# Layer norm 2 and attention weights transposed by DMA instead of TensorE, with held fc1 loads and row-wise weight loads

## The chip, the cores and the metric

The kernel runs on one core of one Trainium2 chip. The metric is the device time of one execution in microseconds (us). The span of a profile is about 1.8 us shorter than the time of the same run. Engines: PE (TensorE matmuls), DVE (VectorE), ACT (ScalarE), POOL (GpSimd), SP (SyncE, which issues the loads).

## The reference

One diffusion-transformer block, in bf16, with B = 2 sequences of N = 256 tokens, D = 1152, two heads and an MLP of F = 4608:

```python
h = layernorm(x) * (1 + scale_a) + shift_a
q, k, v = split(h @ wqkv)
attn = softmax(q @ k.T * Dh ** -0.5)
x = x + gate_a * ((attn @ v) @ wo)
h2 = layernorm(x) * (1 + scale_m) + shift_m
return x + gate_m * (gelu(h2 @ w_fc1) @ w_fc2)
```

The shifts, scales and gates come from `silu(c) @ w_mod`. The 512 tokens are four token tiles of 128 (t = 0, 1 are b = 0; t = 2, 3 are b = 1). D is nine blocks of 128, numbered k. This kernel lays the dimension that a matmul sums over on the partitions. So the attention weights and the normalized h2, which are made with tokens on the partitions, are transposed before they enter attention-times-V and fc1: 16 and 36 blocks of 128 x 128.

## The kernel before

The parts that matter, cut. Weight matrices are loaded as column panels (runs of 768 B) or, for `w_mod`, as groups of rows (runs of 2304 B), in pieces of 864 KB. SP issues the loads in order, each when its buffer is free (the longest wait of a load for PE in the trace is 15.5 us):

```python
def load_section(name, s):                       # row-wise
    for r in range(0, KD, 3):
        nc.sync.dma_start(w[:, r:r + 3, :], wmod_v[:, r:r + 3, s * D:(s + 1) * D])
def load_panels(name, view, col0):               # column panels, PW = 384
    for n in range(NPD):
        nc.sync.dma_start(w[:, :, n * PW:(n + 1) * PW], view[:, :, col0 + n * PW:...])
```

Attention weights are transposed on PE, 16 blocks of 128 x 128, then copied out of PSUM:

```python
for b in range(B):
    for h in range(H):
        pTt = acc_tile([P, TPB, N], "pTt", BF16)
        for qt in range(TPB):
            for kc in range(TPB):
                nc.tensor.transpose(pTt[:, kc, ...], attn_tiles[(b, h, qt)][...], ident[:])
        evac(attnT, pTt[:])
```

Layer norm 2: statistics of x1 on DVE, normalization on ACT and DVE, then 36 transposes on PE that are mixed as "filler" among the wo matmuls (for b = 0) and the fc1 matmuls (for b = 1). The modulation (scale and shift per feature) is done while PSUM is drained:

```python
def ln2_transpose(b, ks, eng):
    pt = aux_tile([P, len(ks), N], "pt", BF16)
    ...  nc.tensor.transpose(pt[:, i, ...], xn2[b * TPB + tl][:, k * P:(k + 1) * P], ident[:])
    ...  # ACT or DVE: hT[:, k, b] = pt * scale_m[k, b] + shift_m[k, b]
```

fc1 works on the first MSPLIT = 10 of its 36 output blocks once for b = 0 (256 columns), then once for b = 1, so that it can start while b = 1 is still being normalized. The other blocks take all 512 tokens at once.

## Time and profile before

| | before |
|---|---|
| time, median of runs | 250.13 us |
| attention-times-V starts | 77.88 us |
| wo starts | 82.24 us |
| fc1 starts | 100.79 us |
| fc2 starts | 174.41 us |
| span ends | 248.30 us |

The stage starts are those of the first matmul of each stage in the trace. First the page of the kernel before: the span, PE's busy time with its share of the span and number of instructions, and the shares of the chain of waits that ended last.

```profile
span 248.3 us, 4032 instructions
...
PE 239.7 (97%) x1734; PEld 144.9 (58%) x1745; DVE 63.9 (26%) x172; ACT 69.1 (28%) x135; POOL 30.8 (12%) x46
...
PE 91%; DMA 3%; ACT 2%; DVE 1%; issue 1%; SPq 0%; ACTq 0%; DVEq 0%
```

PE is busy for 97% of the span and makes up 91% of the chain. By this chain only work taken off PE, or a PE wait removed, can shorten this kernel. Next the timeline of the kernel before at the end of the V stage (start us, duration us, engine, line, operation, tiles, count).

```profile
76.33 0.65 PE L488 MATMUL pacc<-w_v,hT 128*128 128x384 bf16 x3
...
76.81 1.06 PE L523 MATMUL pTt<-ident,soft 128*128 128x128 bf16 x16
...
77.88 0.38 PE L544 MATMUL pa<-soft,big_136 128*128 128x256 bf16 x2
```

Between the last V matmul and the first attention-times-V matmul (L544) stand 16 transposes, 1.07 us from the first of them to L544. The layer-norm-2 transposes among the wo matmuls, from the same view:

```profile
96.21 0.39 PE L582 MATMUL pt<-ident,xn 128*128 128x128 bf16 x4
...
96.44 0.98 PE L611 MATMUL pacc<-w_o,big_136 128*128 128x384 bf16 x5
...
97.25 0.39 PE L582 MATMUL pt<-ident,xn 128*128 128x128 bf16 x4
```

One period of four transposes and five wo matmuls is 97.25 - 96.21 = 1.04 us. Undisturbed wo matmuls follow each other every 0.163 us, so five take about 0.81 and four transposes about 0.22. A transpose costs PE about 0.055 us (the starts of successive ones in a group are 0.056 us apart), not the 0.1 us that its row suggests, because the spans drawn for matmuls overlap (the row of four is drawn to 96.60, the wo matmul after it begins at 96.44). One group of four, at 109.38 us, also waits. From the table of PE's waits (total us, times, longest us):

```profile
PE pt L582 <- ACT hT L587: 1.0, 1, 1.0
```

Together about 4 us, 1.6% of the run, can be gained here at most.

### The profile page before, as it was taken

The page shows a single profiled execution, that of the slowest core. Times are in us where ns is not written, and L with a number is a line of the kernel's source. Part 1 is how long each engine was busy: PE and PEld are TensorE (multiplying, and loading weights), DVE is VectorE, ACT ScalarE, POOL GpSimd, SP SyncE. Part 2 cuts the span into 40 slices and gives each one's busy share as a digit, 9 for nine tenths or more (in the row PEclk, how much of TensorE's full clock was granted, in tenths as well). Part 3 has the DMA queues.
Part 4 walks back from the last instruction along what each step waited for, and adds up shares of the span by engine and source line. Part 5 has one row for each costly group of instructions (what it writes and reads, how often), then busy time and mean ns, then how long its engine had stood idle before and what let it go on. Part 6 is the DMA issues. An engine that isn't in the chain of part 4 may idle for free.

```text
span 248.3 us, 4032 instructions
## 1 busy us (share of the span) xinstructions
PE 239.7 (97%) x1734; PEld 144.9 (58%) x1745; DVE 63.9 (26%) x172; ACT 69.1 (28%) x135; POOL 30.8 (12%) x46
## 2 busy tenths in 40 slices
PE   6799999999999999989999999999999999999994
PEld 2585444456657656878744444444565666656674
DVE  2852551335535588720001000000001100000001
ACT  7641341252424325593224222332000000000000
POOL 4000000021000255100003010000011122211111
PEclk9999999999999999999999999999999999999999
DMA  6999999999999999993194997490000000000000
GB/s 231 326 337 364 365 334 386 331 370 394 372 327 328 326 329 326 326 372 148 33 338 109 338 340 227 141 288 1 0 16 18 16 16 18 17 16 20 26 22 17
DMA packets 54285, 51.59 MB, mean 208 GB/s; under 512 B 1515, under 2 KB 47995, under 8 KB 54267
## 3 DMA queue, kind: packets, MB, share of 16 engines
q1 hardware_dynamic: 53664, 50.14, 64.0%
q0 software_dynamic: 576, 1.19, 1.4%
q8 instruction: 13, 0.21, 0.4%
q14 instruction: 5, 0.04, 0.1%
q10 hardware_dynamic: 27, 0.00, 0.0%
HBM read 50.14 MB, written 1.19 MB: 207 GB/s over the span
## 4 chain that ended last, share of the span: by engine, by line
PE 91%; DMA 3%; ACT 2%; DVE 1%; issue 1%; SPq 0%; ACTq 0%; DVEq 0%
PE pacc L704 28%; PE pacc L658 25%; PE pacc L488 7%; PE pacc L611 7%; PE pacc L436 7%; PE pk L265 5%; DMA w_scale_a<-in_w_mod_dram 3%; PE pk L298 2%; PE pa L544 2%; PE ps_s L464 2%; PE pn L381 1%; PE pg L414 1%; PE pm L233 1%; PE pt L243 1%; PE pt L582 1%
## 5 line engine op out<-in xcount | busy, mean ns | idle before, releaser
L704 PEld LDWEIGHTS <-gT 128*128 128x128 bf16 x468 | 44.4, 98 | 26.2
L710 DVE TENSOR_TENSOR tmp<-pacc,gate 128x384 f32<-128x384 f32 (+2 forms) x13 | 6.9, 527 | 103.8 <-PE pacc L704 103.8
L682 ACT ACTIVATE gT<-pacc 128x512 bf16<-128x512 f32 x26 | 15.5, 597 | 34.9 <-PE pacc L658 34.9
L712 POOL TENSOR_TENSOR o_sb<-tmp,x_1139 128x384 bf16<-128x384 f32 (+1 forms) x12 | 11.7, 972 | 88.9 <-DVE tmp L710 88.9
L488 PE MATMUL pacc<-w_v,hT 128*128 128x384 bf16 x108 | 19.2, 326 | 0.0
L704 PE MATMUL pacc<-w_f_2_1852,gT 128*128 128x384 bf16 (+2 forms) x117 | 18.9, 314 | 0.0
L658 PE MATMUL pacc<-hT,w_f_0_128 128*128 128x256 bf16 x162 | 18.8, 273 | 0.0
L704 PE MATMUL pacc<-w_f_1_1750,gT 128*128 128x384 bf16 x108 | 18.7, 326 | 0.0
L611 PE MATMUL pacc<-w_o,big_136 128*128 128x384 bf16 x108 | 18.5, 326 | 0.0
L704 PE MATMUL pacc<-w_f_3_1954,gT 128*128 128x384 bf16 (+2 forms) x135 | 18.4, 294 | 0.0
L704 PE MATMUL pacc<-w_f_0_1622,gT 128*128 128x384 bf16 x108 | 18.2, 326 | 0.0
L658 PE MATMUL pacc<-hT,w_f_1_132 128*128 128x512 bf16 (+1 forms) x88 | 17.9, 357 | 0.1
L436 PE MATMUL pacc<-hT,w_q 128*128 128x512 bf16 x79 | 17.7, 379 | 0.1
L658 PE MATMUL pacc<-hT,w_f_3_1047 128*128 128x512 bf16 x80 | 17.6, 379 | 0.1
L658 PE MATMUL pacc<-hT,w_f_2_1043 128*128 128x512 bf16 x79 | 17.5, 379 | 0.1
L658 PEld LDWEIGHTS <-w_f_0_128 128*128 128x128 bf16 x162 | 15.7, 98 | 1.8
L425 POOL DMA_DIRECT2D gates_dram<-nat x8 | 4.3, 543 | 79.6 <-DVE nat L422 79.6
L618 POOL TENSOR_TENSOR x_1139<-tmp,x_sb 128x384 f32<-128x384 f32 x11 | 10.0, 912 | 33.1 <-issue 27.0
L488 PEld LDWEIGHTS <-hT 128*128 128x128 bf16 x108 | 10.4, 98 | 6.3 <-issue 0.5
L611 PEld LDWEIGHTS <-big_136 128*128 128x128 bf16 x108 | 10.4, 98 | 6.2
L265 PE MATMUL pk<-big_136,w_k 128*128 128x256 bf16 (+2 forms) x88 | 13.3, 292 | 0.5 <-ACT big_136 L252 0.4
L658 PEld LDWEIGHTS <-w_f_1_132 128*128 128x128 bf16 x90 | 8.7, 98 | 8.5 <-issue 0.3
(119 smaller groups left out, 220.2 us busy)
## 6 DMA issues: line engine op xcount, KB each, us to landing
w_shift_a<-in_w_mod_dram SPq DMA_DIRECT2D x3, 864.0 KB, 11.1
w_q<-in_wqkv_dram SPq DMA_DIRECT2D x3, 864.0 KB, 12.3
w_gate_a<-in_w_mod_dram SPq DMA_DIRECT2D x3, 864.0 KB, 10.0
w_v<-in_wqkv_dram SPq DMA_DIRECT2D x3, 864.0 KB, 12.4
w_shift_m<-in_w_mod_dram SPq DMA_DIRECT2D x3, 864.0 KB, 10.2
w_scale_m<-in_w_mod_dram SPq DMA_DIRECT2D x3, 864.0 KB, 14.8
w_o<-in_wo_dram SPq DMA_DIRECT2D x3, 864.0 KB, 16.4
w_f_0_128<-in_w_fc_dram SPq DMA_DIRECT2D x3, 864.0 KB, 10.3
```

What stands on the lines that cost most here:

```text
L265: nc.tensor.matmul(pk[m][:, c0:c1], w_k[:, k, m * P:(m + 1) * P], hT0[:, k, c0:c1], start=(k == 0 and c0 == 0), stop=(k == KD - 1), skip_g ...
L298: nc.tensor.matmul(pk[m][:], w_k[:, k, m * P:(m + 1) * P], hT0[:, k, :], start=(k == 0), stop=(k == KD - 1),)
L436: nc.tensor.matmul(pacc[:], w_q[:, k, m * P:(m + 1) * P], hT[:, k, :], start=(k == 0), stop=(k == KD - 1),)
L464: nc.tensor.matmul(ps_s[:], qT[:, cc, q0:q0 + P], k_ap, start=(i == 0), stop=(i == len(chunks) - 1),)
L488: nc.tensor.matmul(pacc[:], hT[:, k, t * P:(t + 1) * P], w_v[:, k, pnl * PW:(pnl + 1) * PW], start=(k == 0), stop=(k == KD - 1),)
L611: nc.tensor.matmul(pacc[:], aT[:, k, t * P:(t + 1) * P], w_o[:, k, c0:c1], start=(k == 0), stop=(k == KD - 1),)
L618: (nc.gpsimd if pool_add else nc.vector).tensor_tensor(x1[:, t, c0:c1], tmp[:], x_sb[:, t, c0:c1], op=ALU.add)
L658: nc.tensor.matmul(dst, w_f1[m // KD][:, k, ml * P:(ml + 1) * P], hT[:, k, c0:c1], start=(k == 0), stop=(k == KD - 1),)
L682: nc.scalar.activation(gT[:, m, :], pacc[:], ACT.Gelu_apprx_tanh)
L704: nc.tensor.matmul(pacc[:], gT[:, kk, t * P:(t + 1) * P], w_f2[j][:, r, c0 - n * PW:c0 - n * PW + cw], start=(kk == 0), stop=(kk == KF - 1),)
L710: nc.vector.tensor_tensor(tmp[:], pacc[:], gate_m[:, b, c0:c0 + cw], op=ALU.mult)
L712: (nc.vector if last else nc.gpsimd).tensor_tensor(o_sb[:], tmp[:], x1[:, t, c0:c0 + cw], op=ALU.add)
```

## The change

The transposes leave PE: eight DMA transposes, issued from ACT's queue, take their place (four of 128 KB for attention during the V stage, four of 288 KB, one for each token tile, in layer norm 2). What is then modulated lies in SBUF, and DVE does it in place. The fc1 loads are made to wait, so that they do not run beside a transpose: the first two tiles until attention-times-V has begun, the other two until the last transpose has landed. Loads become row-wise. MSPLIT becomes 12, and the first six blocks of fc1 go step by step over k, so that fc1 can start when only k = 0 is modulated. Smaller moves: a Gelu on one column before fc1, the last residual add of each token tile on DVE, the normalization of token tile 1 split over ACT and DVE, the gate of the MLP made later. The core of the diff, cut:

```diff
-    w_v = load_panels("w_v", wqkv_v, 2 * D)
+    w_v = load_rows("w_v", wqkv_v, 2 * D)
 ... (w_o and the fc1 tiles likewise; w_q stays in panels)
+    def attn_transpose(i):
+        pair = attn_all[:, TPB * i:TPB * (i + 1), :].rearrange("p i n -> p (i n)")
+        nc.scalar.dma_start_transpose(attnT_all[:, i, :]..., pair)
 ... (called in the V loop; the transposes on PE and their copies are removed)
+            if b == 0 and cp == cpairs[0]:
+                tc.add_manual_dep(first_load["w_f1_0"], av.ins.name, WAIT_FOR, ...)
+    def ln2_modulate(b, k):
+        h = hT[:, k, b * N:(b + 1) * N]
+        return nc.vector.tensor_scalar(h, h, scale_m[...], shift_m[...], op0=ALU.mult, op1=ALU.add)
     def ln2_normalize(t, split, between):
         ...  # Sqrt on ACT
+        for k in between:
+            ln2_modulate(0, k)
         ...  # reciprocal, nb, normalization on DVE and ACT
+        nc.scalar.dma_start_transpose(hT[:, :, t * P:(t + 1) * P], xn2[:])
-    def ln2_transpose(b, ks, eng): ...
+    BETWEEN = {2: (0, 1), 3: (5,)}
     for o, (t, i) in enumerate(order):
+        if o == len(order) - 1:
+            ln2_modulate(0, 2)
+            ln2_modulate(0, 3)
+        wo_group(t, i, i < NPD - 1)
         if o:
             ln2_stats(*order[o - 1])
+    ln2_modulate(0, 4)
     ln2_stats(*order[-1])
+    for k in range(6, KD):
+        ln2_modulate(0, k)
-    MSPLIT = 10
+    MSPLIT = 12
 ... (fc1: k-stepped over six blocks, then the other six block by block)
+            mods = [ln2_modulate(1, k) for k in range(KD)]
+            tc.add_manual_dep(first_load["w_f1_2"], mods[0].ins.name, WAIT_FOR, ...)
```

More of the change, by code (lines that the diff above doesn't have):

```diff
@@ L49 @@
     ORDER_ONLY = mybir.DependencyInfo(mybir.DependencyClass.NoSync, mybir.DependencyReason.DATA)
+    WAIT_FOR = mybir.DependencyInfo(mybir.DependencyClass.Sync, mybir.DependencyReason.DATA)
     first_traced = len(nc.cur_bb.bb.instructions)
@@ L107, with load_rows @@
     nc.sync.dma_start(w_k[:, :, KM1 * P:D], wqkv_v[:, :, D + KM1 * P:2 * D])
-    def load_section(name, s):
+    first_load = {}
+    def load_rows(name, view, col0):
         w = wide_tile(name)
         for r in range(0, KD, 3):
-            nc.sync.dma_start(w[:, r:r + 3, :], wmod_v[:, r:r + 3, s * D:(s + 1) * D])
+            load = nc.sync.dma_start(w[:, r:r + 3, :], view[:, r:r + 3, col0:col0 + D])
+            first_load.setdefault(name, load.ins)
         return w
@@ L119, in load_panels @@
         return w
-    w_shift_a = load_section("w_shift_a", S_SHIFT_A)
+    w_shift_a = load_rows("w_shift_a", wmod_v, S_SHIFT_A * D)
     w_q = load_panels("w_q", wqkv_v, 0)
-    w_gate_a = load_section("w_gate_a", S_GATE_A)
-    w_v = load_panels("w_v", wqkv_v, 2 * D)
-    w_shift_m = load_section("w_shift_m", S_SHIFT_M)
-    w_scale_m = load_section("w_scale_m", S_SCALE_M)
-    w_o = load_panels("w_o", wo_v, 0)
+    w_gate_a = load_rows("w_gate_a", wmod_v, S_GATE_A * D)
+    w_v = load_rows("w_v", wqkv_v, 2 * D)
+    w_shift_m = load_rows("w_shift_m", wmod_v, S_SHIFT_M * D)
+    w_scale_m = load_rows("w_scale_m", wmod_v, S_SCALE_M * D)
+    w_o = load_rows("w_o", wo_v, 0)
     w_f1 = [None] * 4
-    w_f1[0] = load_panels("w_f1_0", wfc1_v, 0)
-    w_f1[1] = load_panels("w_f1_1", wfc1_v, D)
+    w_f1[0] = load_rows("w_f1_0", wfc1_v, 0)
+    w_f1[1] = load_rows("w_f1_1", wfc1_v, D)
     big1 = act.tile([P, 4 * KD, T], BF16, name="big1", tag="big")
@@ L451 @@
     attn_all = soft[:, 2 * n_s * N:3 * n_s * N].rearrange("p (i n) -> p i n", n=N)
-    attnT_all = soft[:, 3 * n_s * N:4 * n_s * N].rearrange("p (i c n) -> p i c n", c=TPB, n=N)
+    attnT_all = soft[:, 3 * n_s * N:4 * n_s * N].rearrange("p (i n) -> p i n", n=2 * N)
     attn_tiles = {}
@@ L496, in v_group @@
             evac(v4m[:, t, 1, HP:P], pacc[:, c4 + HP:c4 + P])
+    def attn_transpose(i):
+        pair = attn_all[:, TPB * i:TPB * (i + 1), :].rearrange("p i n -> p (i n)")
+        nc.scalar.dma_start_transpose(attnT_all[:, i, :].rearrange("p (c n) -> p c n", n=P), pair)
     score_order = [(b, h, qt) for b in range(B) for h in range(H) for qt in range(TPB)]
@@ L505 @@
             fin()
+        if i >= 2 and i % 2 == 0 and i // 2 <= B * H:
+            attn_transpose(i // 2 - 1)
         if i == 8:
@@ L510, with attnT @@
             nc.vector.tensor_scalar_add(scale_m[:, :, 0:B], scale_m[:, :, 0:B], 1.0)
-    w_f1[2] = load_panels("w_f1_2", wfc1_v, 2 * D)
-    w_f1[3] = load_panels("w_f1_3", wfc1_v, 3 * D)
-    w_gate_m = load_section("w_gate_m", S_GATE_M)
-    attnTs = {}
-    for b in range(B):
-        for h in range(H):
-            pTt = acc_tile([P, TPB, N], "pTt", BF16)
-            for qt in range(TPB):
-                for kc in range(TPB):
-                    nc.tensor.transpose(
-                        pTt[:, kc, qt * P:(qt + 1) * P],
-                        attn_tiles[(b, h, qt)][:, kc * P:(kc + 1) * P], ident[:],
-                    )
-            attnT = attnT_all[:, b * H + h, :, :]
-            evac(attnT, pTt[:])
-            attnTs[(b, h)] = attnT
+    w_f1[2] = load_rows("w_f1_2", wfc1_v, 2 * D)
+    w_f1[3] = load_rows("w_f1_3", wfc1_v, 3 * D)
+    w_gate_m = load_rows("w_gate_m", wmod_v, S_GATE_M * D)
+    def attnT(b, h, kc):
+        blocks = attnT_all[:, b * H + h, :].rearrange("p (q c n) -> p c q n", c=TPB, n=P)
+        return blocks[:, kc, :, :]
     cpairs = [(0, 1), (2, 3), (4, 5), (6, 7), (8,)]
@@ L536 @@
                 if cc == HC:
-                    srcs = [(v4m[:, b * TPB + kc, h, :], attnTs[(b, h)][:, kc, :])
+                    srcs = [(v4m[:, b * TPB + kc, h, :], attnT(b, h, kc))
                             for h in range(H) for kc in range(TPB)]
@@ L540, with ln2_normalize @@
                     h = 0 if cc < HC else 1
-                    srcs = [(v_sb[:, b * TPB + kc, cc * P:(cc + 1) * P], attnTs[(b, h)][:, kc, :])
+                    srcs = [(v_sb[:, b * TPB + kc, cc * P:(cc + 1) * P], attnT(b, h, kc))
                             for kc in range(TPB)]
                 for i, (lhsT, rhs) in enumerate(srcs):
-                    nc.tensor.matmul(
-                        pa[:, ci, :], lhsT, rhs, start=(i == 0), stop=(i == len(srcs) - 1),
-                    )
+                    av = nc.tensor.matmul(
+                        pa[:, ci, :].rearrange("p (q n) -> p q n", n=P), lhsT, rhs, start=(i == 0), stop=(i == len(srcs) - 1),
+                    )
+            if b == 0 and cp == cpairs[0]:
+                tc.add_manual_dep(first_load["w_f1_0"], av.ins.name, WAIT_FOR, reason="transposes first")
             evac(aT[:, cp[0]:cp[0] + len(cp), b * N:(b + 1) * N], pa[:])
-    fill, fill_state = [], [0, 1]
-    def filler():
-        fill_state[0] += 1
-        if fill and fill_state[0] >= fill_state[1]:
-            fill_state[0] = 0
-            fill.pop(0)()
     x1 = act.tile([P, NT, D], FP32, name="x1", tag="x1")
     mv2 = small.tile([P, NT, 2], FP32, name="mv2", tag="mv2", bufs=1)
-    xn2 = [None] * NT
-    def ln2_normalize(t, split):
+    def ln2_modulate(b, k):
+        h = hT[:, k, b * N:(b + 1) * N]
+        return nc.vector.tensor_scalar(
+            h, h, scale_m[:, k, b:b + 1], shift_m[:, k, b:b + 1], op0=ALU.mult, op1=ALU.add,
+        )
+    def ln2_normalize(t, split, between):
         rstd = small.tile([P, 1], FP32, name="rstd", tag="rstd")
         nc.scalar.activation(rstd[:], mv2[:, t, 1:2], ACT.Sqrt, bias=eps_t[:], scale=1.0)
+        for k in between:
+            ln2_modulate(0, k)
         nc.vector.reciprocal(rstd[:], rstd[:])
@@ L568, in ln2_normalize @@
         nc.vector.tensor_scalar(nb[:], mv2[:, t, 0:1], rstd[:], -1.0, op0=ALU.mult, op1=ALU.mult)
-        xn2[t] = work.tile([P, D], BF16, name="xn", tag="xn", bufs=4)
+        xn2 = work.tile([P, D], BF16, name="xn", tag="xn", bufs=4)
         cs = 5 * P if split else D
-        nc.scalar.activation(xn2[t][:, 0:cs], x1[:, t, 0:cs], ACT.Identity, bias=nb[:], scale=rstd[:])
         if cs < D:
             nc.vector.tensor_scalar(
-                xn2[t][:, cs:D], x1[:, t, cs:D], mv2[:, t, 0:1], rstd[:],
+                xn2[:, cs:D], x1[:, t, cs:D], mv2[:, t, 0:1], rstd[:],
                 op0=ALU.subtract, op1=ALU.mult,
             )
-    def ln2_transpose(b, ks, eng):
-        pt = aux_tile([P, len(ks), N], "pt", BF16)
-        for i, k in enumerate(ks):
-            for tl in range(TPB):
-                nc.tensor.transpose(
-                    pt[:, i, tl * P:(tl + 1) * P], xn2[b * TPB + tl][:, k * P:(k + 1) * P], ident[:]
-                )
-        for i, k in enumerate(ks):
-            if eng == "a":
-                nc.scalar.activation(
-                    hT[:, k, b * N:(b + 1) * N], pt[:, i, :], ACT.Identity,
-                    bias=shift_m[:, k, b:b + 1], scale=scale_m[:, k, b:b + 1],
-                )
-            else:
-                nc.vector.tensor_scalar(
-                    hT[:, k, b * N:(b + 1) * N], pt[:, i, :], scale_m[:, k, b:b + 1], shift_m[:, k, b:b + 1],
-                    op0=ALU.mult, op1=ALU.add,
-                )
-    def fill_ln2(b, every):
-        fill.extend(
-            lambda i=i: ln2_transpose(b, range(2 * i, min(2 * i + 2, KD)), "ad"[i % 2])
-            for i in range((KD + 1) // 2)
-        )
-        fill_state[:] = [0, every]
+        nc.scalar.activation(xn2[:, 0:cs], x1[:, t, 0:cs], ACT.Identity, bias=nb[:], scale=rstd[:])
+        nc.scalar.dma_start_transpose(hT[:, :, t * P:(t + 1) * P], xn2[:])
     stats2 = [small.tile([P, NPD, 6], FP32, name="stats2", tag="stats2") for _ in range(NT)]
@@ L614, in wo_group @@
             )
-            filler()
         tmp = work.tile([P, PW], FP32, name="tmp", tag="tmp", bufs=3)
@@ L625, in ln2_stats @@
             nc.vector.bn_aggr(mv2[:, t, :], stats2[t][:].rearrange("p a b -> p (a b)"))
-            if t != NT - 2:
-                ln2_normalize(t, t == NT - 1)
+            ln2_normalize(t, t % 2 == 1, BETWEEN.get(t, ()))
     order = [(t, i) for t in range(NT) for i in range(NPD)]
     for o, (t, i) in enumerate(order):
-        if (t, i) == (3, 0):
-            fill_ln2(0, 5)
-        wo_group(t, i, o < len(order) - 1)
+        if o == len(order) - 1:
+            ln2_modulate(0, 2)
+            ln2_modulate(0, 3)
+        wo_group(t, i, i < NPD - 1)
         if o:
             ln2_stats(*order[o - 1])
-    while fill:
-        fill.pop(0)()
-    ln2_normalize(NT - 2, False)
+    ln2_modulate(0, 4)
     ln2_stats(*order[-1])
+    for k in range(6, KD):
+        ln2_modulate(0, k)
     w_f2 = []
@@ L654, with f1_mm @@
     gT = act.tile([P, KF, T], BF16, name="gT", tag="big")
-    def f1_mm(dst, m, k, c0, c1):
+    def f1_mm(dst, m, k, c0, c1, start, **kw):
         ml = m % KD
@@ L659, in f1_mm @@
             dst, w_f1[m // KD][:, k, ml * P:(ml + 1) * P], hT[:, k, c0:c1],
-            start=(k == 0), stop=(k == KD - 1),
+            start=start, stop=(k == KD - 1), **kw,
         )
-    MSPLIT = 10
+    MSPLIT = 12
+    early_gelu = small.tile([P, 1], FP32, name="early_gelu", tag="early_gelu", bufs=1)
+    nc.scalar.activation(early_gelu[:], zeros[:, 0:1], ACT.Gelu_apprx_tanh)
     for b in range(B):
-        for m0 in range(0, MSPLIT, 2):
-            pacc = acc_tile([P, 2, N], "pacc")
-            for m in (m0, m0 + 1):
-                for k in range(KD):
-                    if b == 0 and m * KD + k == 40:
-                        fill_ln2(1, 8)
-                    f1_mm(pacc[:, m - m0, :], m, k, b * N, (b + 1) * N)
-                    filler()
-            nc.scalar.activation(gT[:, m0:m0 + 2, b * N:(b + 1) * N], pacc[:], ACT.Gelu_apprx_tanh)
-        while fill:
-            fill.pop(0)()
+        for stepped in (True, False):
+            ms = range(0, MSPLIT // 2) if stepped else range(MSPLIT // 2, MSPLIT)
+            accs = {m0: acc_tile([P, 2, N], "pacc") for m0 in ms[::2]} if stepped else {}
+            steps = [(m, k) for k in range(KD) for m in ms] if stepped else [(m, k) for m in ms for k in range(KD)]
+            for m, k in steps:
+                m0 = m - m % 2
+                if m0 not in accs:
+                    accs[m0] = acc_tile([P, 2, N], "pacc")
+                f1_mm(accs[m0][:, m - m0, :], m, k, b * N, (b + 1) * N, start=(k == 0 and m == m0), skip_group_check=True)
+                if k == KD - 1 and m == m0 + 1:
+                    nc.scalar.activation(
+                        gT[:, m0:m0 + 2, b * N:(b + 1) * N], accs[m0][:], ACT.Gelu_apprx_tanh,
+                    )
+        if b == 0:
+            mods = [ln2_modulate(1, k) for k in range(KD)]
+            tc.add_manual_dep(first_load["w_f1_2"], mods[0].ins.name, WAIT_FOR, reason="transposes first")
     gate_m = None
@@ L680 @@
         for k in range(KD):
-            f1_mm(pacc[:], m, k, 0, T)
+            f1_mm(pacc[:], m, k, 0, T, k == 0)
         nc.scalar.activation(gT[:, m, :], pacc[:], ACT.Gelu_apprx_tanh)
-        if m == 14:
+        if m == 22:
             gate_m = gate_natural(1, w_gate_m)
```

## The prediction

> **What bounds it.** PE. The page gives PE 239.7 of 248.3 us (97%) and the chain of waits 91% PE, at full granted clock. The timeline shows what else PE does from attention to fc1:
> - 16 attention transposes from 76.7 us, about 0.9 us before the first attention-times-V matmul;
> - 36 layer-norm-2 transposes. A block of four plus five wo matmuls repeats every 1.04 us, so four cost about 0.22 us, all 36 about 2.0 us;
> - one PE gap of 0.99 us at 108.4, a transpose waiting for ACT to drain its PSUM tile.
>
> That is about 4 us, 1.6%, nearly all the change can win.
>
> **What the change adds and moves.**
> - MSPLIT 12 instead of 10: 36 matmuls of 256 columns replace 18 of 512. At 0.109 against 0.216 us each that is free.
> - Row-wise loads (2304 B instead of 768 B runs). Landings of 864 KB pieces are 2.25 us apart row-wise, 2.7 us for panels, about 390 against 327 GB/s. [...] PE waits for no DMA after 8.7 us, so this gives slack, not time. w_v, now needed whole at V (52.8), should land at 52.2; w_o, needed at 81, near 75.
> - fc1 loads held to about 77: the first two tiles should land by 93, needed at 99 and 107. The others, held to about 107, are needed at 134 and 152. No wait.
> - Eight DMA transposes, four of 128 KB and four of 288 KB, issued from ACT. The 96 KB stores took 1.6 us from issue to landing; small transfers beside bulk loads 5 to 8 us. [...] My estimate from both: [...] the attention ones in 5 to 8 beside loads.
>
> **Critical path.** Attention transposes are issued near 58, 63, 67, 71 us and needed at 77 (first two) and 79: hidden, if the last takes under 8 us. In layer norm 2, the transpose of token tile 1 is issued about 95.1 us; fc1 could start at 99.0. On DVE the modulates of k = 0, 1 stand before the normalization of tile 2, so a latency over about 2.3 us stalls DVE and delays the modulates k = 2 to 8, which the k-stepped fc1 needs 0.65 us apart. With 4 us latency I get about 2.5 us of PE waits in the first 6 us of fc1 for b = 0; b = 1 is covered. So: gain 4.2, give back 2.5, net about 2 us.
>
> **Time: 248.3 us, 80% in 245.8 to 251.5.** Faster by over 2%: 0.05; within 2%: 0.88; slower by over 2%: 0.07.
>
> **Right if:** PE busy falls by about 3 to 4 us; the 0.99 us gap is gone; new PE waits in fc1 name DVE's modulates or the transposes, 1 to 4 us in sum; no PE wait at V, attention or wo; row-wise landings 2.2 to 2.3 us apart; large transposes land in 3 to 5 us.
>
> **Wrong if:** a large transpose takes 7 us or more, each us then costing one; issuing transposes blocks ACT for several us, so that PSUM runs out; transposes slow the loads of w_o beyond 81 us; or the latency is near 2 us, when almost the whole 4 us is kept (about 246).

Two passages with hardware figures and rules that no trace or run of this case shows are cut from this text, and with them the estimate drawn in part from one: 3 to 5 us to landing for the large transposes. The "4 us latency" is the middle of that estimate, so it was an assumption of mine that no trace had shown. The sum itself: 4.2 us gained less 2.5 given back is 1.7, rounded to "about 2", which takes 250.13 us to about 248.3.

## The result, and the profile after

The changed kernel takes 248.32 us (median of 4 runs, 248.14 to 248.87) against 250.13 us (249.99 to 250.68). The ratio is 0.9927, 95% interval 0.9905 to 0.9949: within 2%, and clear of noise.

| first matmul of the stage, us | before | after | difference |
|---|---|---|---|
| attention-times-V | 77.88 | 76.83 | -1.05 |
| wo | 82.24 | 81.19 | -1.05 |
| fc1 | 100.79 | 98.74 | -2.05 |
| fc2 | 174.41 | 172.49 | -1.92 |
| end of span | 248.30 | 246.37 | -1.93 |

So 1.05 us are gained in front of attention-times-V and 1.00 us in the wo stage. In fc1, where another 18 transposes and the PE wait of 1 us have gone, nothing is gained: fc1 lasts 73.62 us before and 73.75 us after. The page of the changed kernel:

```profile
span 246.4 us, 3980 instructions
...
PE 238.0 (97%) x1700; PEld 143.9 (58%) x1711; DVE 67.0 (27%) x184; ACT 62.5 (25%) x124; POOL 28.0 (11%) x43
...
PE 88%; DVE 7%; DMA 2%; ACT 1%; issue 1%; DVEq 0%; ACTq 0%
```

The chain now runs over DVE for 7% of the span, where it was 1%. The timeline of the changed kernel where attention-times-V begins, with no transposes left between:

```profile
75.36 1.64 PE L492 MATMUL pacc<-w_v,hT 128*128 128x384 bf16 x9
...
76.83 1.04 PE L545 MATMUL pa<-soft,big 128*128 128x256 bf16 x8
```

PE's waits in the changed kernel:

```profile
PE pacc L637 <- DVE hT L559: 1.5, 3, 0.6
```

L637 is fc1's matmul and L559 the modulate on DVE. The wait of L582 is gone; this one is new. The timeline of the changed kernel around the start of fc1 shows it. In brackets stand the engine's idle time before the row and what ended it.

```profile
94.84 1.32 ACTq L579 DMA_TRANSPOSE hT<-xn  x1
...
98.14 0.60 DVE L559 TENSOR_SCALAR hT<-hT,scale_m,shift_m 128x256 bf16<-128x256 bf16 x2 [0.24 <-DMA hT<-xn]
...
98.74 1.47 PE L637 MATMUL pacc<-hT,w_f 128*128 128x256 bf16 x12
...
98.97 0.55 DVE L593 TENSOR_TENSOR tmp<-pacc,gate 128x384 f32<-128x384 f32 x1
...
99.44 0.55 DVE L602 BATCH_NORM_STATS2 stats<-x 128x6 f32<-128x384 f32 x1
...
99.91 0.95 DVE L559 TENSOR_SCALAR hT<-hT,scale_m,shift_m 128x256 bf16<-128x256 bf16 x2
...
100.66 1.47 PE L637 MATMUL pacc<-hT,w_f 128*128 128x256 bf16 x12 [0.44 <-DVE hT L559]
...
101.83 0.55 DVE L602 BATCH_NORM_STATS2 stats<-x 128x6 f32<-128x384 f32 x1
...
102.31 0.33 DVE L559 TENSOR_SCALAR hT<-hT,scale_m,shift_m 128x256 bf16<-128x256 bf16 x1
...
102.69 1.75 PE L637 MATMUL pacc<-hT,w_f 128*128 128x256 bf16 x12 [0.56 <-DVE hT L559]
...
104.07 0.54 DVE L574 TENSOR_SCALAR xn<-x,mv,rstd 128x512 bf16<-128x512 f32 x1
...
104.92 1.25 PE L637 MATMUL pacc<-hT,w_f 128*128 128x256 bf16 x10 [0.48 <-DVE hT L559]
```

The transpose of token tile 1 lands at 98.04, DVE waits 0.24 us for it, and fc1 starts on time. Then PE needs a new k every 0.65 us (six matmuls of 0.109 us), but DVE evicts a wo tile and takes statistics between the modulates of k = 1 and k = 2, and again between k = 3, 4 and 5; between k = 5 and 6 it normalizes token tile 3. From the start of one matmul to the start of the next, four places take 0.71, 0.84, 0.39 and 0.75 us where an undisturbed step takes 0.109: 2.25 us lost. (The table of waits shows only 1.5 of it, since the end of a matmul is drawn about 0.16 us after the next could start: 0.273 us long, 0.109 us apart.) The transposes themselves, of layer norm 2 (L579) and of attention (L505), in the changed kernel, times from issue to landing:

```profile
L579 ACTq DMA_TRANSPOSE hT<-xn x4: 1260/1300/1317, 90.8 to 105.2; - x4
...
DMA to landing us min/median/max: 3.2/3.2/4.8
```

```profile
L505 ACTq DMA_TRANSPOSE soft<-soft x4: 1220/1238/1352, 58.5 to 70.5; - x4
...
DMA to landing us min/median/max: 7.2/9.4/10.0
```

The large ones, with the loads held back, land after 3.2 us, except the first (4.8), which still has the last fc1 loads beside it. With no load packet beside them, tiles 1 to 3 move their first packet 1.2 us after the issue and all 288 KB in the next 1.54 to 1.57 us, 188 to 191 GB/s (the expectation of e1 below says about 150). The attention ones are less than half the size and run beside the loads of `w_scale_m` and `w_o`: 7.2 to 10.0 us. They are hidden all the same. The last lands at 77.7, when b = 1 needs it at about 79.

### The profile page after: what moved, and what is told of

It reads as the page before. It is cut to its first block, busy times and chain, and to the rows that moved or that the text cites. A ratio compares the mean times of both kernels' runs of the same rounds, so it can differ in the third digit from the quotient of the medians.

```text
span 246.4 us, 3980 instructions
## 1 busy us (share of the span) xinstructions
PE 238.0 (97%) x1700; PEld 143.9 (58%) x1711; DVE 67.0 (27%) x184; ACT 62.5 (25%) x124; POOL 28.0 (11%) x43
## 4 chain that ended last, share of the span: by engine, by line
PE 88%; DVE 7%; DMA 2%; ACT 1%; issue 1%; DVEq 0%; ACTq 0%
PE pacc L691 29%; PE pacc L637 27%; PE pacc L492 7%; PE pacc L440 7%; PE pk L269 4%; PE pk L302 2%; PE pwarm L162 2%; PE pacc L588 2%; PE pa L545 2%; PE ps_s L468 2%; DVE stats L602 2%; PE pn L385 1%; DVE tmp L593 1%; DMA hT<-xn 1%; PE pg L418 1%; DMA c_sb<-in_c_dram 1%
## 5 line engine op out<-in xcount | busy, mean ns | idle before, releaser
L637 PE MATMUL pacc<-hT,w_f 128*128 128x256 bf16 (+1 forms) x427 | 70.9, 325 | 1.9 <-DVE hT L559 1.5
L691 PE MATMUL pacc<-w_f,gT 128*128 128x384 bf16 (+2 forms) x468 | 70.5, 314 | 0.0
L637 PEld LDWEIGHTS <-w_f 128*128 128x128 bf16 x432 | 42.1, 98 | 30.1 <-issue 2.5
L699 POOL TENSOR_TENSOR o_sb<-tmp,x 128x384 bf16<-128x384 f32 (+1 forms) x12 | 11.7, 971 | 73.8 <-DVE tmp L697 73.8
L588 PE MATMUL pacc<-w_o,big 128*128 128x384 bf16 x108 | 17.7, 326 | 0.0
L588 PEld LDWEIGHTS <-big 128*128 128x128 bf16 x108 | 10.6, 98 | 6.9
L269 PE MATMUL pk<-big,w_k 128*128 128x256 bf16 (+2 forms) x88 | 13.3, 292 | 0.5 <-ACT big L256 0.4
L440 PEld LDWEIGHTS <-w_q 128*128 128x128 bf16 x81 | 7.8, 98 | 9.7 <-DMA w_q<-in_wqkv_dram 0.3
L594 POOL TENSOR_TENSOR x<-tmp,x_sb 128x384 f32<-128x384 f32 x8 | 7.3, 914 | 35.9 <-DVE tmp L593 35.9
L269 PEld LDWEIGHTS <-w_k 128*128 128x128 bf16 x90 | 7.5, 97 | 3.4 <-DMA w_k<-in_wqkv_dram 0.3
```

The lines of the kernel that those rows point to most:

```text
L269: nc.tensor.matmul(pk[m][:, c0:c1], w_k[:, k, m * P:(m + 1) * P], hT0[:, k, c0:c1], start=(k == 0 and c0 == 0), stop=(k == KD - 1), skip_g ...
L440: nc.tensor.matmul(pacc[:], w_q[:, k, m * P:(m + 1) * P], hT[:, k, :], start=(k == 0), stop=(k == KD - 1),)
L588: nc.tensor.matmul(pacc[:], aT[:, k, t * P:(t + 1) * P], w_o[:, k, c0:c1], start=(k == 0), stop=(k == KD - 1),)
L594: (nc.gpsimd if pool_add else nc.vector).tensor_tensor(x1[:, t, c0:c1], tmp[:], x_sb[:, t, c0:c1], op=ALU.add)
L637: nc.tensor.matmul(dst, w_f1[m // KD][:, k, ml * P:(ml + 1) * P], hT[:, k, c0:c1], start=start, stop=(k == KD - 1), **kw,)
L691: nc.tensor.matmul(pacc[:], gT[:, kk, t * P:(t + 1) * P], w_f2[j][:, r, c0 - n * PW:c0 - n * PW + cw], start=(kk == 0), stop=(kk == KF - 1),)
```

## The experiments

Theory A: the gain is the PE time of the transposes, about 4.2 us; half of it is given back because DVE delivers the modulates late at the start of fc1; the holds are what keeps the transposes short. Rivals: B, the holds are only caution; C, the latency of the transposes, not DVE, makes the stalls. All nine kernels gave correct results, and all are timed against the kernel before in the same batch.

### e1_no_hold and e2_second_free: are the holds needed?

```diff
-                tc.add_manual_dep(first_load["w_f1_0"], av.ins.name, WAIT_FOR, ...)    # e1 only
-            tc.add_manual_dep(first_load["w_f1_2"], mods[0].ins.name, WAIT_FOR, ...)   # e1 and e2
```

> Changed kernel without the two holds on the fc1 loads. Theory A (a DMA transpose beside bulk loads gets only a small share of the DMA engines: in the changed kernel's trace its 256 B packets moved 15 to 40 GB/s beside loads and about 150 GB/s alone): the attention transposes no longer end at 77.7 us but later, and the four large ones, now beside fc1 loads until about 103 us, take 8 us or more to land instead of 3.2; fc1 waits for them, 252 to 260 us. Rival B (the holds are caution[...]): landings within 1.5 us of the changed kernel's, time within 0.5% of 248.3.

> Only the second hold is taken away (third and fourth fc1 tile follow the second at once). Attention is as in the changed kernel, so the wo stage starts at 81.2 as there. Theory A: the transposes of token tiles 1 to 3, alone on the DMA engines before, now land in 6 us or more, and fc1 waits 3 us or more longer: 251 to 256 us. Rival B: 3.2 to 4 us to landing and 248 to 249 us.

Measured: e1 262.60 us (ratio 1.0493, 1.0477 to 1.0509), e2 261.74 us (1.0457, 1.0441 to 1.0473). Rival B falls. My numbers for theory A were too mild as well; both times lie above the range. The first hold was not taken away by itself: e1, which lacks both, is 0.9 us slower than e2, and PE waits 0.7 us in it for an attention transpose, so most of the loss comes with the second. From e2: the layer-norm-2 transposes from issue to landing, and PE's wait.

```profile
L579 ACTq DMA_TRANSPOSE hT<-xn x4: 1302/2212/5692, 91.0 to 118.5; - x4
...
DMA to landing us min/median/max: 3.3/9.4/16.3
```

```profile
PE pacc L637 <- DVE hT L559: 12.8, 1, 12.8
```

The transpose of tile 0 takes 12.8 us and that of tile 1 16.3 us. The latter lands only after the last fc1 load, at 111.3, and fc1 waits for it. The packets of e2's trace show two parts of this. First, tile 0's transpose moves no packet for 3.95 us after its issue, where a transpose of the changed kernel with no load beside it waits 1.2 us; tile 1's packets begin only when tile 0's end, at 103.0. The first attention transpose of the changed kernel, with loads beside it, also waits 4.0 us (58.50 to 62.51). Why the first packet comes so late, no run here shows. Second, the packets then come slowly. From 97 to 107 us the load queue moved 1508 packets of 2304 B and the transpose queue 1539 packets of 256 B, about one for one. Equal counts give the transposes 256 / (256 + 2304) = 10% of the bytes, and that is what they got: 39 GB/s beside 348 GB/s of loads. The attention transposes of the changed kernel show the same: from 68 to 71 us 454 packets of 256 B, 39 GB/s, beside 440 of 2304 B, 338 GB/s. Why the counts are so nearly equal was not shown. The issue was slow then too: that of tile 1 held ACT's queue for 5.7 us instead of 1.3.

In the long wait the clock falls as well. In the busy time of e2 by windows, the columns after the engines are the granted clock, the DMA share and GB/s:

```profile
106.00:112.00 6.00, 0.17 (x1) 0.21 (x2) 0.56 (x3) 0.00 (x0) 0.00 (x0) 0.50 0.85 310
112.00:119.00 7.00, 7.00 (x40) 5.11 (x39) 6.37 (x20) 2.56 (x3) 0.92 (x1) 0.59 0.99 290
```

In the trace PE's clock fell to half at 104.05 us, 5.0 us after the last wo matmul, and came back at 117.70, 5.9 us after fc1's first; from 112 to 119 us it was 0.59 on average. In e1, where PE waits 13.0 us in fc1, it was 0.50 from 105 to 111 us. In the changed kernel, whose waits in fc1 are under 1 us each, the clock stays at 1.00. What sets it was not tested.

### e3_panels and e7_before_rows: what are row-wise loads worth?

```diff
# e3: the changed kernel, panels for w_v, w_o and the fc1 tiles (cut: one of them shown)
-    w_f1[0] = load_rows("w_f1_0", wfc1_v, 0)
+    w_f1[0] = load_panels("w_f1_0", wfc1_v, 0)
# e7: the kernel before, row-wise loads for the same tensors, nothing else (cut: w_q keeps its panels)
-        for n in range(NPD):
-            nc.sync.dma_start(w[:, :, n * PW:(n + 1) * PW], ...)
+        for r in range(0, KD, 3):
+            nc.sync.dma_start(w[:, r:r + 3, :], view[:, r:r + 3, col0:col0 + D])
```

> Changed kernel with column-panel loads (768 B runs) for w_v, w_o and all fc1 tiles, holds kept. At 327 instead of 390 GB/s the held fc1 tiles 0 and 1 end about 97 us instead of 94.7, so the transposes of token tiles 0 and 1 (issued 90.9 and 94.8) have loads beside them longer. If row-wise loads matter through this: tile 1 lands near 100 instead of 98.0, 249 to 251 us. If they only give slack, as I predicted: within 0.3% of 248.3.

> The kernel before with row-wise loads alone for w_v, w_o and the fc1 tiles. PE waits for no load after 8.7 us there, so: no change, 249.8 to 250.4; landings 2.25 us apart instead of 2.7. If the row-wise loads had a share of the gain [...], it would show as 249.5 or less.

Measured: e3 250.57 us (ratio 1.0008, 0.9986 to 1.0029), e7 250.31 us (1.0005, 0.9988 to 1.0022). In the kernel before, the row-wise loads are worth nothing, as PE waits for no load there after 8.7 us. In the changed kernel they are worth all that the change gains: without them it is as slow as the kernel before. In e3 the last held fc1 piece lands at 99.1 us instead of 94.7, and the transposes of tiles 0 and 1 run beside the loads:

```profile
L580 ACTq DMA_TRANSPOSE hT<-xn x4: 1296/1375/2874, 90.8 to 107.5; - x4
...
DMA to landing us min/median/max: 3.2/4.4/8.7
```

The timeline of e3 shows DVE waiting for the transpose of tile 1, and PE for DVE:

```profile
100.48 0.60 DVE L560 TENSOR_SCALAR hT<-hT,scale_m,shift_m 128x256 bf16<-128x256 bf16 x2 [2.63 <-DMA hT<-xn]
...
100.88 1.47 PE L638 MATMUL pacc<-hT,w_f 128*128 128x256 bf16 x12 [2.02 <-DVE hT L560]
```

Tile 1 lands at 100.4 instead of 98.0, and fc1 starts at 100.88 instead of 98.74. This was the first possibility of the expectation; my prediction had stood for the second.

### e5_attn_pe: the attention transposes alone

```diff
-        if i >= 2 and i % 2 == 0 and i // 2 <= B * H:
-            attn_transpose(i // 2 - 1)
+    ... nc.tensor.transpose(pTt[...], attn_tiles[(b, h, qt)][...], ident[:]) ... evac(...)
```

> Changed kernel with the 16 attention transposes back on PE. If the parts add up: the wo stage starts 1.05 us later (82.2), everything else as in the changed kernel, 249.3 us (249.0 to 249.7). The w_o loads, without transposes beside them, land by 75 instead of 77.3.

Measured: 249.09 us (ratio 0.9957, 0.9942 to 0.9972), inside the range. V's first matmul is at 53.09 and attention-times-V's at 78.17, that is 25.08 us later; in the changed kernel it is 24.02 us. The attention part is worth 1.06 us of the span, as the table of stages said. The second w_o piece lands at 71.4 instead of 74.7 us. The loads of e5 were 0.6 us earlier already before the first transpose (w_v), so the four transposes of 128 KB had delayed them by about 2.7 us, more than their bytes would (by my estimate 1.3 us for 512 KB at 390 GB/s). (The landing of the third piece is not in this trace.)

### e9_msplit: is MSPLIT 12 free?

```diff
-    MSPLIT = 10
+    MSPLIT = 12
```

> The kernel before with MSPLIT 12 instead of 10 alone (36 matmuls of 256 columns for 18 of 512). My prediction calls this free: 250.0 to 250.6. Were the weight loads of the narrower matmuls a cost, it would be 18 more of 0.1 us, 252.

Measured: the kernel before with this alone takes 250.22 us (ratio 0.9996, 0.9979 to 1.0013). It is free.

### e6_dummy: what does latency cost?

```diff
+        if t == 1:
+            junk = act.tile([P, KD, P], BF16, name="junk")
+            nc.scalar.dma_start_transpose(junk[:, 0:9, :], xn2[:, 0:9 * P])
         nc.scalar.dma_start_transpose(hT[:, :, t * P:(t + 1) * P], xn2[:])
```

> An extra transpose of the same 288 KB into an unused tile is issued on ACT just before that of token tile 1. Tile 1's issue moves by the 1.3 us that an issue takes and its landing by 1.3 to 3 us. My prediction says that each us of latency beyond about 2.3 costs one, so 249.6 to 251.3 us. Rival: PE is held by DVE's own work in fc1, the latency has slack, under 0.5 us lost (248.3 to 248.8).

Measured: 249.74 us (ratio 0.9978, 0.9963 to 0.9994). Tile 1's transpose lands at 99.62 instead of 98.04, 1.58 us later, and the median is 1.4 us above that of the changed kernel (of another batch). fc1 starts 1.38 us later (100.12 against 98.74) and then has the same four stalls, of 2.46 us in sum instead of 2.25. So the slope of one for one holds. From e6's timeline:

```profile
99.72 0.60 DVE L559 TENSOR_SCALAR hT<-hT,scale_m,shift_m 128x256 bf16<-128x256 bf16 x2 [1.76 <-DMA hT<-xn]
```

But at the latency of the changed kernel this cost is only just beginning: DVE waits 0.24 us there. The 2.25 us of stalls are something else.

### e4_spread and e8_order: DVE's load, or its order?

```diff
# e4 (cut): k = 2, 6, 8 on ACT, 5, 7 on POOL; 0, 1, 3, 4 on DVE, 3 and 4 earlier
-    BETWEEN = {2: (0, 1), 3: (5,)}
+    BETWEEN = {2: ((2, "a"), (0, "d"), (1, "d"))}
+        if o == len(order) - 2:
+            ln2_modulate(0, 3); ln2_modulate(0, 4)          # after wo_group, before ln2_stats
+    ln2_modulate(0, 5, "p"); ln2_modulate(0, 6, "a"); ln2_modulate(0, 7, "p"); ln2_modulate(0, 8, "a")
# e8: all on DVE, only earlier
-    BETWEEN = {2: (0, 1), 3: (5,)}
+    BETWEEN = {2: (0, 1, 2, 3)}
         if o == len(order) - 1:
-            ln2_modulate(0, 2)
-            ln2_modulate(0, 3)
+            for k in range(4, 8):
+                ln2_modulate(0, k)
-    ln2_modulate(0, 4)
+    ln2_modulate(0, 8)
     ln2_stats(*order[-1])
-    for k in range(6, KD):
-        ln2_modulate(0, k)
```

> The modulates of k = 2, 6, 8 (b = 0) go to ACT and 5, 7 to POOL; DVE keeps 0, 1, 3, 4 and runs 3, 4 before the statistics. Theory A (the four fc1 stalls of together 2.25 us, from the starts of successive matmuls, come from DVE's order and load, as DVE waits only 0.24 us for the transpose): stalls fall under 0.8 us, 246.3 to 247.2 us. Rival C (the transpose's latency sets them): no change, 248.3.

> All modulates stay on DVE, only their order changes: k = 0 to 3 before tile 2's normalization, 4 to 7 before the last wo eviction, 8 before the last statistics. If it is the order that starved fc1 (theory A1): the sum of DVE work is the same, the modulates come early enough, tile 3's transpose is issued about 106 instead of 105.2 and lands before fc1 needs it at 110.5; stalls under 0.6 us, 246.1 to 246.9. If it is DVE's load (A2, DVE is busy 5.7 of 6 us there, work must leave it): the delay only moves to the later transposes and the second half, 247.3 to 248.3.

Measured: e4 246.14 us (246.10 to 246.37; ratio 0.9838, 0.9823 to 0.9852), e8 246.29 us (246.03 to 246.65; ratio 0.9837, 0.9822 to 0.9852). Both beat the kernel before by 1.6% and the changed kernel (of another batch) by about 2 us; e4 lies just below its expected range, e8 inside. In both, fc1 lasts 71.51 us instead of 73.75 and has no stall. Rival C falls: in e8 the transpose of tile 1 still takes 3.21 us. e8 also parts the two forms of theory A. From 99 to 105 us, first the changed kernel, then e8 (busy time of PE, weight loads, DVE, ACT, POOL):

```profile
99.00:105.00 6.00, 4.40 (x37) 3.35 (x35) 5.73 (x17) 2.40 (x3) 0.92 (x1) 1.00 0.26 49
```

```profile
99.00:105.00 6.00, 6.00 (x58) 5.38 (x56) 5.53 (x17) 1.64 (x2) 0.92 (x1) 1.00 0.26 49
```

DVE is as full in e8 (5.53 us of 6) as in the changed kernel (5.73), and PE has no idle time. So it was the order, not the load. The timeline of e8:

```profile
98.29 1.11 DVE L559 TENSOR_SCALAR hT<-hT,scale_m,shift_m 128x256 bf16<-128x256 bf16 x4 [0.26 <-DMA hT<-xn]
...
98.88 8.35 PE L635 MATMUL pacc<-hT,w_f 128*128 128x256 bf16 x75
...
100.57 1.46 DVE L559 TENSOR_SCALAR hT<-hT,scale_m,shift_m 128x256 bf16<-128x256 bf16 x4
...
106.37 1.56 ACTq L579 DMA_TRANSPOSE hT<-xn  x1
```

PE runs through without a break. The price is paid where there is slack: tile 3's transpose is issued at 106.4 instead of 105.2 and lands at 109.7, before b = 1 begins at about 110.7 (98.88 and 108 matmuls of 0.109 us).

## Why the prediction was right or wrong

The time was right: 248.3 predicted, 248.32 measured. That it agrees so closely is in part luck, as the second point shows. Point by point:

- **What can be gained, 4.2 us: right.** Measured 1.05 us before attention-times-V, 1.00 us in wo, and 2.11 us in fc1 (73.62 before, 71.51 in e8 with no stall left), together 4.16 us.
- **What is given back, "about 2.5 us of PE waits in the first 6 us of fc1": right in size and place,** 2.25 us. Its cause was half right. I made it hang on the transpose's latency: "With 4 us latency I get about 2.5 us", and "the latency is near 2 us, when almost the whole 4 us is kept". The latency was 3.2 us and cost DVE 0.24 us; the rest was the order of DVE's work behind it. e6 shows that further latency does cost one for one; e8 keeps the latency and loses the stalls. The latency term was over-sized and the order term under-sized, and it was luck that the two errors nearly cancelled.
- **Attention transposes hidden: right.** I expected 5 to 8 us beside loads; they took 7.2 to 10.0, and the last, issued at 70.5, took 7.2, near the limit of 8 that I had set.
- **Row-wise loads give "slack, not time": wrong for the changed kernel.** As the only change they give nothing (e7), but with the holds they decide whether the loads end before the transposes start (e3, about 2.2 us). I had counted the loads' deadlines for PE and not those for the transposes.
- **Held fc1 loads make no wait: right.** The first two tiles landed by 94.7 (predicted 93), the third is first needed after 130 us. w_o landed at 77.3, not near 75, still before 81.2.
- **"PE busy falls by about 3 to 4 us": wrong,** 1.7 us. In the first 52 us the changed kernel shows 48.95 us busy against 48.09, though V starts at the same time in both: the trace before has a wait of 0.9 us for `w_scale_a` that the other lacks, and that comes and goes among the runs. Without that stretch the fall is 2.5 us. The stalls also hide partly inside the drawn matmuls. Busy time was a poor sign; the starts of the stages are a good one.
- **No PE wait at V, attention or wo; the 0.99 us gap gone; MSPLIT free (e9): right.**
- **What I did not price at all** was the absence of the holds. In e1 and e2 the transposes of tiles 0 and 1 beside row-wise loads took 12.8 to 16.7 us.

## What to carry to other kernels

Moving the transposes from PE to DMA paid here only what they had cost PE, 0.055 us each and a wait of 1 us, and it turned an in-order cost into a latency, 3.2 us in quiet: put what the consumer needs first also first on the engine that prepares it, and let work with slack (here the last statistics) come later. Keep bulk loads away from a small transfer that the chain waits for, since in e2 the two queues moved about as many packets but not as many bytes (39 against 348 GB/s), and tile 0's first packet came 3.95 us after the issue; a change that shortens the loads may then be worth something although PE never waited for them (about 2.2 us in e3). Measure where each stage starts rather than sums of busy time.
